# Regrouped columns in tiles of four groups, and batch 0 routed in three parts (512, 1024 and 1024 rows)

## The chip, the cores and the metric

The kernel runs on one core of a Trainium2 chip. The metric is the device time of one execution in microseconds (us), as the median over several runs. A core has a matrix engine (PE, with its weight loads as PEld), a vector engine (DVE), a scalar engine (ACT), a general-purpose engine (POOL) and a queue processor (SP) that issues most transfers. Each engine executes its own instructions strictly in the order of the program and waits for others through semaphores.

## The reference

A Fourier mixing of eight batches, then a mixture of experts in which every row goes to one expert and none is dropped:

```python
X = np.fft.fft(x, axis=1)                 # x: (8, 2496, 256)
x = np.fft.fft(X, axis=2).real.astype(np.float32).reshape(8 * 2496, 256)

logits = x @ w_gate                       # 8 experts
expert_idx = np.argmax(logits, axis=1)
probs = softmax(logits)                   # + 1e-9 in the denominator
gate_w = probs[np.arange(N), expert_idx]
for e in range(8):                        # rows of expert e, w1: (256, 1024), w2: (1024, 256)
    y[rows_e] = np.maximum(x[rows_e] @ w1[e], 0.0) @ w2[e]
return gate_w[:, None] * y
```

## The kernel before, in words

**Transform.** The sequence of 2496 is taken as 104 x 24. `first(b)` does the transforms of length 104 for one batch: it loads the batch in three thirds (`load`, tile `xq`, three buffers), folds each third on DVE (lines 290 to 301), multiplies it on PE (`half1`, PSUM tile `s`), copies the result to SBUF (tile `t`, line 316) and writes it to a scratch array `Td[b]` in DRAM. It has twelve steps. `regroup(b, h)` reads `Td[b]` back with the axes exchanged, as tiles `t4` (the trace calls them `t`). There are eleven groups of 120 columns a batch; before, they come in two tiles, of six groups (768 KB) and five groups (640 KB). `second(b)` does the transforms of length 24 and of the feature axis. Per tile, `turn_last` runs one small matmul (`pr`) and a copy back into `t4` (line 367). Per group, `group` runs two matmuls (the trace calls their PSUM tile `p`, read from `table,t`) and a copy into `zz` (line 374). Then come ten windows of 128 columns: each has two matmuls (PSUM tile `p`, read from `table,zz`), a copy `zs` on ACT (line 400), a copy of the logits `lg` and two operations for 256 finished rows on DVE (lines 403 and 405), and a copy `mirror` on ACT (line 379).

**Routing.** After every half of the windows (five of them, 1280 rows) `route` computes, in 17 small DVE operations, one exponential on ACT and eleven small matmuls (`rk`), the position of every row in a scratch array `Xs` that is sorted by expert. `base` carries the fill of the experts from one part to the next. The rows then wait in a list; each call of `send()` puts one indirect write (128 rows) on POOL's queue (line 230, `Xs<-rows,pi`). A batch needs 20 of them.

**Experts.** `plan` (lines 481 to 514, DVE) turns the fill of the experts into tables of blocks. `experts` is a generator over blocks: `fetch_weights` and `fetch_rows` are issued on SP, `turn` transposes the rows of a block on PE (`pt`, line 571), then come the two products `ph` and `py` (`a` to `e` in a variant with seven products), and POOL writes the rows out. The blocks of round b may start once all rows of batch b have been sent (`whole`). Only then does `fetch_rows` read `Xs`, and it waits for the landing of all indirect writes of that batch.

**Order.** The order of instructions is written out by hand (`tc.manual_schedule()`). After the first stage of batch 0, the program runs the steps of `second(0)` with steps of `early` (the first stage of batch 1) between them and one `send()` after each step; before, seven steps of `early` stand ahead of `second(0)` and one more follows every even step. Then the loop over rounds runs the expert blocks of round b-1 with side steps for batch b: the plan, the second stage of batch b and the first stage of batch b+1. Ahead of the first block lie 18 side steps; they reach the fourth window of batch 1. The PSUM pool `pm_` has three buffers, which `s`, `pr`, `p` and `rk` share.

Of the kernel before, what the change touches and what calls it, by code (L numbers as in the profile page):

```python
# [28 lines left out]
GP = NU * NB  # L29
NP = 112  # L30
NW = -(-NK * NB // 128)
HW = NW // 2
HALF = -(-NG // 2)
LAST = NW * 128 - (NG - 1) * GP
NT = B * S
E, F = 8, 1024
# [2 lines left out]
CAP = NT + BLK  # L39
ROWS = E * CAP + BLK  # L40
W = D + 2
NSL = 2 * HW
NY = H + 1
OUT = 1.0e6

# [11 lines left out]
def shape_consts():  # L57

    c = {}
    n1 = np.arange(NA)[:, None]  # L60
    r = np.arange(NP)
    k1 = r // 2
    im = r % 2

    def wave(n2, f):
        return f(2 * np.pi / S * ((NB * n1 + n2) * k1 % S))

    w1 = [np.where(im, wave(n2, np.sin), wave(n2, np.cos)) for n2 in range(1, NS)]
    for f in (np.cos, np.sin):
        w1 += [np.where(im, 0.0, wave(0, f)), np.where(im, wave(NS, f), 0.0)]  # L70
    c["w1"] = np.stack(w1, 1) * (k1 < NK)

    u, cs, s = np.meshgrid(np.arange(NU), np.arange(2), np.arange(NS), indexing="ij")
    u, cs, s = (v.reshape(-1, 1) for v in (u, cs, s))
    k2 = np.arange(NB)
    t = 2 * np.pi / NB * ((s + 1) * k2 % NB)
    end = np.where(cs, 1.0 - 2.0 * (k2 % 2), 1.0)
    even = np.where(s == NS - 1, end, np.where(cs, -np.sin(t), np.cos(t)))
    odd = np.where(s == NS - 1, end, np.where(cs, np.cos(t), np.sin(t)))
    own = (u == np.arange(NU)).astype(float)  # L80
    c["m2"] = np.stack([(own[:, :, None] * m[:, None, :]).reshape(GP, GP) for m in (even, odd)], 1)

    rot = np.zeros((GP, GP))
    for p in range(GP):
        if p % NS == NS - 1:
            rot[p, p] = 1.0
        elif p // NS % 2:
            rot[p, p - NS] = -1.0
        else:
            rot[p, p + NS] = 1.0  # L90
    c["rot"] = rot

    d = np.arange(H)[:, None]
    m = np.arange(D + 1)
    t = 2 * np.pi / D * (d * m % D)
    rc, rs = np.cos(t), -np.sin(t)
    rs[0] = 1.0 - 2.0 * (m % 2)
    full = np.concatenate([rc[:, :D], rs[:, :D]], 0)


    rd = np.zeros((H, 2, 2 * E + NY + 1))
    sign = 1.0 - 2.0 * (m[:NY] % 2)
    rd[:, 0, 0:NY] = sign * rc[:, 0:NY]
    rs[0] = 0.0
    rd[0, 1, 2 * E] = 1.0
    rd[:, 1, 2 * E + 1:] = sign * rs[:, 0:NY]
    c["rd"] = rd
    c["alt"] = 1.0 - 2.0 * (np.arange(128) % 2)[:, None]
    c["rt"] = full.T.reshape(2, 128, D).transpose(1, 0, 2)

    p = np.arange(128)[:, None, None, None]
    h = np.arange(2)[None, :, None, None]
    g = np.arange(HW)[None, None, :, None]
    mir = np.arange(2)
    tau = 128 * (HW * h + g) + p
    k1 = tau // NB
    k = k1 + NA * (tau % NB)
    bad = (k1 >= NK) | ((mir == 1) & ((k1 == 0) | (k1 == NK - 1)))
    row = np.where(bad, 0, np.where(mir, S - k, k))
    c["row"] = row.reshape(128, 2, NSL)  # L120
    c["good"] = 1.0 - bad.reshape(128, 2, NSL)
    c["far"] = OUT * bad.reshape(128, 2, NSL)
    c["rev"] = np.broadcast_to(E - np.arange(E), (128, E))
    c["cap"] = np.broadcast_to(CAP * np.arange(E), (128, E))
    c["sgn"] = np.where(np.arange(128) == 0, 1.0, -1.0)[:, None]
    c["lane"] = np.arange(128)[:, None]
    c["tri"] = np.triu(np.ones((128, 128)), 1)
    c["ident"] = np.eye(128)
    return {n: np.ascontiguousarray(v, dtype=np.float32) for n, v in c.items()}
# [50 lines left out]
    return todo  # L180


TICKS = 32
LATE = 4
SHARE, ROOM = 0.6, 1.2
# [24 lines left out]
def kernel(ctx: ExitStack, tc, x, w_gate, w1, w2, out):  # L210
# [3 lines left out]
    def mm(o, lhsT, rhs, start=True, stop=True, **kw):  # L214
        nc.tensor.matmul(o, lhsT=lhsT, rhs=rhs, start=start, stop=stop, **kw)  # L215
# [128 lines left out]
    base = con["cap"]  # L344

    def regroup(b, h):
        t4 = sp.tile([128, HALF, D], F32, tag="t4", name="t4")
        n = min(HALF, NG - h * HALF)
        nc.sync.dma_start(
            out=t4[:, 0:n], in_=bass.AP(Td[b].tensor, Td[b].offset + h * HALF * GP * D,  # L350
                                        [[D, 128], [GP * D, n], [1, D]]))
        ahead[b, "t4", h] = t4

# [2 lines left out]
    def second(b):  # L356
# [3 lines left out]
        def turn_last(h):  # L360

            nonlocal t4
            t4 = ahead.pop((b, "t4", h))
            n = min(HALF, NG - h * HALF)
            pr = pm_.tile([GP, HALF], F32, tag="m", name="pr")
            mm(pr[:, 0:n], con["rot"][:], t4[0:GP, 0:n, H])
            act.copy(t4[0:GP, 0:n, H], pr[:, 0:n])  # L367

        def group(g):
            i, n = g % HALF, LAST if g == NG - 1 else GP  # L370
            p2 = pm_.tile([128, 2, n], F32, tag="m", name="p2")
            for c in range(2):
                mm(p2[:, c], t4[0:GP, i, c * H:(c + 1) * H], con["m2"][:, c, 0:n])
            act.copy(zz[:, :, g * GP:g * GP + n], p2[:])
            if g == HALF - 1:
                turn_last(1)

        def mirror(rows, k):
            act.copy(free(rows[:], (k + 1) * W + D - 1, [-W, 2], [-1, H - 1]),
# [5 lines left out]
        yield  # L385
        group(1)
        yield
        for h in range(2):
            rows = sp.tile([128, NSL, W], F32, tag="rows", name="rows")
            lg = sp.tile([128, NSL, E], F32, tag="lg", name="lg")  # L390
            for i in range(HW):
                w, k = HW * h + i, 2 * i
                if w + 2 < NG:
                    group(w + 2)
                p3 = pm_.tile([128, 2 * NY + 2 * E + 1], F32, tag="m", name="p3")
# [8 lines left out]
                for m, op in enumerate((ALU.add, ALU.subtract)):  # L404
                    vec.scalar_tensor_tensor(rows[:, k + m, 0:NY], p3[:, 0:NY], zs[:, 0:1], zs[:, 1:],  # L405
                                             op0=ALU.add, op1=op)
                yield
            mirror(rows, k)
            yield from route(b, h, rows, lg)

    def route(b, h, rows, lg):

        nonlocal base

        def small(name, *dims, dt=F32):
            return sp.tile([128, *dims], dt, tag=name, name=name)

        mx, eq, v = small("mx", NSL), small("eq", NSL, E), small("v", NSL)
        vec.reduce_max(mx[:], lg[:], axis=AX_X)
        vec.tensor_tensor(eq[:], lg[:], bc(mx[:], 2, E), op=ALU.is_equal)  # L420
        vec.tensor_tensor(eq[:], eq[:], bc(con["rev"][:], 1, NSL), op=ALU.mult)
        vec.reduce_max(v[:], eq[:], axis=AX_X)
        vec.tensor_tensor(v[:], v[:], con["good"][:, h], op=ALU.mult)
        oh = small("oh", NSL + 1, E, dt=BF16)
        vec.memset(oh[:, NSL], 0.0)
        vec.tensor_tensor(oh[:, 0:NSL], bc(con["rev"][:], 1, NSL), bc(v[:], 2, E), op=ALU.is_equal)
        yield

        su = small("su", NSL)
        vec.tensor_tensor(lg[:], lg[:], bc(mx[:], 2, E), op=ALU.subtract)  # L430
        act.activation(lg[:], lg[:], ACTF.Exp)
        vec.tensor_scalar(rows[:, :, D], con["row"][:, h], float(b * S), None, op0=ALU.add)
        yield

        rk = pm_.tile([128, NSL + 1, E], F32, tag="m", name="rk")
        mm(rk[:], tri[:], oh[:], True, False)
        for s in range(NSL):
            mm(rk[:, s + 1:], ones[:], bc(oh[:, s], 1, NSL - s), False, s == NSL - 1)
        vec.reduce_sum(su[:], lg[:], axis=AX_X)
        vec.tensor_scalar(su[:], su[:], 1e-9, None, op0=ALU.add)  # L440
        vec.reciprocal(rows[:, :, D + 1], su[:])
        yield

        pos, pf, pi = small("pos", NSL, E), small("pf", NSL), small("pi", NSL, dt=I32)
        vec.tensor_tensor(pos[:], rk[:, 0:NSL], bc(base[:], 1, NSL), op=ALU.add)
        vec.tensor_tensor(pos[:], pos[:], oh[:, 0:NSL], op=ALU.mult)
        vec.reduce_sum(pf[:], pos[:], axis=AX_X)
        vec.tensor_tensor(pf[:] if b >= LATE else pi[:], pf[:], con["far"][:, h], op=ALU.add)
        nxt = cp.tile([128, E], F32, tag="base", name="base", bufs=2)
        vec.tensor_tensor(nxt[:], rk[:, NSL], base[:], op=ALU.add)  # L450
        base = nxt
        for s in range(NSL):
            waiting.append((b, pf[:, s:s + 1], pi[:, s:s + 1], rows[:, s]))

    waiting = deque()
# [302 lines left out]
    def ahead_of(b):  # L758

        yield from first(b)  # L760
        regroup(b, 0)
        regroup(b, 1)

    def mixed(b):

# [32 lines left out]
    load(1, 1)  # L798
    regroup(0, 0)
    regroup(0, 1)  # L800
    load(1, 2)
    nc.sync.dma_start(out=bt[:], in_=const_dram("blocks", cv))
    sent(unordered(nc.sync.dma_start(
# [10 lines left out]
        else:  # L814
            vec.tensor_copy(con["rd"][:, c, to + E:to + 2 * E], pg[:])
    early = ahead_of(1)
    for _ in range(7):
        next(early)
    for k, _ in enumerate(second(0)):
        if k % 2 == 0:  # L820
            next(early, None)
        send()
    work = experts(todo)
# [81 lines left out]
```

## Time and profile before

| what | value |
|---|---|
| median of 7 runs | 1322.09 us (1318.71 to 1324.41) |
| the profiled execution | 1321.24 us |
| its span, first to last instruction | 1319.5 us |
| PE busy | 1273.3 us (96%) |
| DVE / ACT / POOL busy | 581.7 / 374.0 / 329.5 us |
| mean granted PE clock | 0.979 |
| first transposition of expert rows (`pt`) | at 85.69 us |

The profiled execution lasts 1.74 us longer than its span and lies 0.85 us below the median. In the lists of the profile each line is a group of instructions: start, duration, engine, source line, operation, output<-input; in square brackets stands the idle time of the engine ahead of it and what ended it. Matmuls in single precision appear as two instructions each.

### The profile page before, as it was taken

What the parts mean: (1) busy time and instruction counts of PE and PEld (TensorE: products, weight loads), DVE (VectorE), ACT (ScalarE), POOL (GpSimd) and SP (SyncE); (2) the same over time, 40 slices, a digit from 0 to 9 for tenths busy, and PEclk for the clock granted to TensorE, in tenths of its full rate; (3) what the DMA queues carried; (4) which work ended last, traced back from release to release, by engine and by line L of the source; (5) the groups of instructions that cost most, each with busy time, mean ns of one, the idle gap of its engine ahead of it and who ended that gap; (6) DMA issues with size and microseconds to landing.
All of it is one profiled execution on the core that took longest, in us unless ns stands there. A gap on an engine that the chain in (4) does not pass through costs nothing.

```text
span 1319.5 us, 19014 instructions
## 1 busy us (share of the span) xinstructions
PE 1273.3 (96%) x6655; PEld 1102.3 (84%) x6655; DVE 581.7 (44%) x1533; ACT 374.0 (28%) x886; POOL 329.5 (25%) x335
## 2 busy tenths in 40 slices
PE   6769999999999999999999999999999999999998
PEld 4649988776888888888888888888888889999887
DVE  4554253352656535655556643675544421111111
ACT  1422141231244223433334322433322221111111
POOL 0236125043114411143113511153311111111111
PEclk6879999999999999999999999999999999999999
DMA  8878967455436522574333632243422237776784
GB/s 235 271 250 294 393 208 246 161 172 197 169 134 213 189 104 100 177 265 147 125 110 99 225 119 100 100 176 132 164 107 105 102 146 273 253 277 255 270 316 189
DMA packets 63100, 249.63 MB, mean 189 GB/s; under 512 B 10057, under 2 KB 24883, under 8 KB 43420
## 3 DMA queue, kind: packets, MB, share of 16 engines
q1 hardware_dynamic: 46231, 203.33, 43.9%
q0 software_dynamic: 15888, 42.14, 8.8%
q10 hardware_dynamic: 885, 2.94, 0.7%
q8 instruction: 54, 0.88, 0.3%
q14 instruction: 42, 0.34, 0.1%
HBM read 194.97 MB, written 54.83 MB: 189 GB/s over the span
## 4 chain that ended last, share of the span: by engine, by line
PE 89%; issue 2%; DMA 1%; POOL 1%; DVE 1%; ACT 0%; POOLq 0%; SPq 0%; ACTq 0%
PE py L215 41%; PE ph L215 14%; PE a L215 7%; PE c L215 7%; PE p L215 5%; PE d L215 3%; PE b L215 3%; PE e L215 3%; PE pt L571 3%; PE s L215 2%; POOL Xs L230 1%; DMA Xs<-rows,pi 1%; DMA xb<-Xs 0%; PE rk L215 0%; ACT y L721 0%
## 5 line engine op out<-in xcount | busy, mean ns | idle before, releaser
L215 PE MATMUL py<-w_sb,hT 128*128 128x256 f32 x2560 | 578.0, 380 | 0.0
L215 PEld LDWEIGHTS py<-w_sb,hT 128*128 128x128 f32 x2560 | 478.0, 191 | 60.2
L230 POOL DMA_INDIRECT out_dram<-y,ro x163 | 159.3, 977 | 811.8 <-ACT y L721 737.9
L215 PE MATMUL ph<-xT,w_sb 128*128 128x128 f32 (+2 forms) x1216 | 220.3, 338 | 2.9 <-ACT y L721 2.1
L721 ACT ACTIVATE y<-py,xb 128x256 f32<-128x256 f32 x163 | 77.2, 474 | 511.6 <-PE py L215 501.8
L215 PEld LDWEIGHTS ph<-xT,w_sb 128*128 128x128 f32 x1216 | 179.2, 192 | 33.6 <-issue 17.2
L230 POOL DMA_INDIRECT Xs<-rows,pi x160 | 162.1, 1013 | 172.7 <-DVE rows L405 53.4
L698 DVE TENSOR_SCALAR hT<-ph 128x512 f32<-128x512 f32 x63 | 43.5, 691 | 297.1 <-issue 204.9
L604 DVE TENSOR_TENSOR u<-p,b 128x512 f32<-128x512 f32 x50 | 34.4, 687 | 172.1 <-PE b L215 156.6
L215 PE MATMUL a<-xT,w_sb 128*128 128x256 f32 x400 | 102.7, 379 | 0.0
L572 DVE TENSOR_SCALAR xT<-pt,table 128x512 f32<-128x512 f32 (+1 forms) x94 | 63.2, 673 | 49.4 <-PE pt L571 49.3
L215 PEld LDWEIGHTS a<-xT,w_sb 128*128 128x128 f32 x400 | 75.5, 190 | 10.0
L215 PE MATMUL s<-xq,w 104*112 104x256 f32 (+2 forms) x208 | 62.0, 421 | 12.1 <-DVE xq L292 11.6
L700 ACT ACTIVATE hT<-ph 128x512 f32<-128x512 f32 x63 | 37.6, 597 | 115.9 <-PE ph L215 115.9
L614 ACT ACTIVATE hT<-a 128x512 f32<-128x512 f32 x50 | 29.9, 597 | 130.9 <-PE a L215 130.9
L403 DVE COPY lg<-p 128x16 f32<-128x16 f32 x80 | 13.8, 173 | 120.2 <-ACT zs L400 120.2
L571 PE MATMUL pt<-table,xb 128*128 128x128 f32 x326 | 53.3, 279 | 9.4 <-DMA xb<-Xs 9.4
L215 PE MATMUL p<-table,zz 128*128 128x145 f32 (+1 forms) x320 | 56.5, 300 | 5.5 <-DVE rows L405 4.3
L215 PEld LDWEIGHTS p<-table,t 120*128 120x128 f32 x352 | 53.5, 201 | 8.9 <-issue 2.4
L571 PEld LDWEIGHTS pt<-table,xb 128*128 128x128 f32 x326 | 39.0, 142 | 24.2 <-DMA xb<-Xs 10.1
L215 PE MATMUL p<-table,t 120*128 120x120 f32 (+1 forms) x352 | 57.5, 287 | 1.6 <-ACT t L367 1.1
L215 PEld LDWEIGHTS s<-xq,w 104*112 104x112 f32 x208 | 38.8, 204 | 22.7 <-DVE xq L292 10.9
(115 smaller groups left out, 1289.6 us busy)
## 6 DMA issues: line engine op xcount, KB each, us to landing
w_sb<-in_moe_w_dram SPq DMA_DIRECT2D x132, 1024.0 KB, 7.7
xq<-in_x_dram SPq DMA_DIRECT2D x24, 896.0 KB, 8.9
xb<-Xs SPq DMA_DIRECT2D x28, 516.0 KB, 3.7
Td<-t SPq DMA_DIRECT2D x18, 448.0 KB, 3.3
t<-Td SPq DMA_DIRECT2D x8, 768.0 KB, 12.4
t<-Td SPq DMA_DIRECT2D x8, 640.0 KB, 14.0
xb<-Xs SPq DMA_DIRECT2D x13, 258.0 KB, 3.0
xb<-Xs SPq DMA_DIRECT2D x25, 129.0 KB, 3.2
```

Of the source, the lines that this page charges most:

```text
L215: nc.tensor.matmul(o, lhsT=lhsT, rhs=rhs, start=start, stop=stop, **kw)
L230: return unordered(pool.indirect_dma_start(out=dst, out_offset=bass.IndirectOffsetOnAxis(ap=idx, axis=0), in_=rows, in_offset=None, bounds ...
L403: vec.tensor_copy(lg[:, k:k + 2], p3[:, NY:NY + 2 * E].rearrange("p (m e) -> p m e", m=2))
L571: nc.tensor.transpose(pt[:, c, t], xb[:, 2 * h + t, c * 128:(c + 1) * 128], ident[:])
L572: vec.tensor_scalar(xT[:, :, 256 * h:256 * h + 128 * n], pt[:].rearrange("p c t k -> p c (t k)"), con["alt"][:], None, op0=ALU.mult)
L604: vec.tensor_tensor(u2[:], p1[:], b[:], op=add)
L614: act.activation(h11, a[:], ACTF.Relu)
L698: vec.tensor_scalar(o, ph[:], 0.0, None, op0=ALU.max)
L700: act.activation(o, ph[:], ACTF.Relu)
L721: act.activation(y[:], py[:], ACTF.Copy, scale=xb[:, i, D + 1:D + 2])
```

## The change

The regrouped columns come in tiles of four groups (`TG = 4`): three transfers a batch, of 512, 512 and 384 KB, into three buffers of the smaller size, with one `turn_last` for each tile, so three instead of two. Batch 0 is routed in three parts, of two, four and four windows (`PARTS`), where all other batches keep two parts of five. `route` takes the size of its part. The constants `row`, `good` and `far` lose the axis for the half and are cut by column. Six steps of `early` stand ahead of `second(0)` instead of seven, and the even steps 0 and 2 of `second(0)` are no longer followed by one.

```diff
-HALF = -(-NG // 2)
+TG = 4
...
+PARTS = (2, 4, 4)
...
     def regroup(b, h):
-        t4 = sp.tile([128, HALF, D], F32, tag="t4", name="t4")
-        n = min(HALF, NG - h * HALF)
+        t4 = sp.tile([128, TG, D], F32, tag="t4", name="t4", bufs=3)
+        n = min(TG, NG - h * TG)
         nc.sync.dma_start(
-            out=t4[:, 0:n], in_=bass.AP(Td[b].tensor, Td[b].offset + h * HALF * GP * D,
+            out=t4[:, 0:n], in_=bass.AP(Td[b].tensor, Td[b].offset + h * TG * GP * D,
                                         [[D, 128], [GP * D, n], [1, D]]))
...
-            if g == HALF - 1:
-                turn_last(1)
+            if g % TG == TG - 1:
+                turn_last(g // TG + 1)
...
-        for h in range(2):
+        w = 0
+        for part in PARTS if b == 0 else (NW // 2, NW // 2):
             rows = sp.tile([128, NSL, W], F32, tag="rows", name="rows")
             lg = sp.tile([128, NSL, E], F32, tag="lg", name="lg")
-            for i in range(HW):
-                w, k = HW * h + i, 2 * i
+            for i in range(part):
+                k = 2 * i
...
+                w += 1
                 yield
             mirror(rows, k)
-            yield from route(b, h, rows, lg)
+            yield from route(b, slice(2 * (w - part), 2 * w), rows[:, 0:2 * part], lg[:, 0:2 * part])
...
-    def route(b, h, rows, lg):
+    def route(b, at, rows, lg):
         nonlocal base
+        n = at.stop - at.start
...
-        rk = pm_.tile([128, NSL + 1, E], F32, tag="m", name="rk")
+        rk = pm_.tile([128, n + 1, E], F32, tag="m", name="rk")
         mm(rk[:], tri[:], oh[:], True, False)
-        for s in range(NSL):
-            mm(rk[:, s + 1:], ones[:], bc(oh[:, s], 1, NSL - s), False, s == NSL - 1)
+        for s in range(n):
+            mm(rk[:, s + 1:], ones[:], bc(oh[:, s], 1, n - s), False, s == n - 1)
...
-        for s in range(NSL):
+        for s in range(n):
             waiting.append((b, pf[:, s:s + 1], pi[:, s:s + 1], rows[:, s]))
...
     def ahead_of(b):
         yield from first(b)
-        regroup(b, 0)
-        regroup(b, 1)
+        for h in range(-(-NG // TG)):
+            regroup(b, h)
...
     regroup(0, 0)
     regroup(0, 1)
+    regroup(0, 2)
     load(1, 2)
...
     early = ahead_of(1)
-    for _ in range(7):
+    for _ in range(6):
         next(early)
     for k, _ in enumerate(second(0)):
-        if k % 2 == 0:
+        if k % 2 == 0 and k >= 4:
             next(early, None)
         send()
```

More of the change, by code (lines that the diff above doesn't have):

```diff
@@ L31 @@
 NW = -(-NK * NB // 128)
-HW = NW // 2
-HALF = -(-NG // 2)
+TG = 4
 LAST = NW * 128 - (NG - 1) * GP
@@ L41 @@
 W = D + 2
-NSL = 2 * HW
+NSL = 2 * (NW // 2)
 NY = H + 1
@@ L109, in shape_consts @@
     c["rt"] = full.T.reshape(2, 128, D).transpose(1, 0, 2)
-    p = np.arange(128)[:, None, None, None]
-    h = np.arange(2)[None, :, None, None]
-    g = np.arange(HW)[None, None, :, None]
+    p = np.arange(128)[:, None, None]
     mir = np.arange(2)
-    tau = 128 * (HW * h + g) + p
+    tau = 128 * np.arange(NW)[None, :, None] + p
     k1 = tau // NB
@@ L119, in shape_consts @@
     row = np.where(bad, 0, np.where(mir, S - k, k))
-    c["row"] = row.reshape(128, 2, NSL)
-    c["good"] = 1.0 - bad.reshape(128, 2, NSL)
-    c["far"] = OUT * bad.reshape(128, 2, NSL)
+    c["row"] = row.reshape(128, 2 * NW)
+    c["good"] = 1.0 - bad.reshape(128, 2 * NW)
+    c["far"] = OUT * bad.reshape(128, 2 * NW)
     c["rev"] = np.broadcast_to(E - np.arange(E), (128, E))
@@ L363, in turn_last @@
             t4 = ahead.pop((b, "t4", h))
-            n = min(HALF, NG - h * HALF)
-            pr = pm_.tile([GP, HALF], F32, tag="m", name="pr")
+            n = min(TG, NG - h * TG)
+            pr = pm_.tile([GP, TG], F32, tag="m", name="pr")
             mm(pr[:, 0:n], con["rot"][:], t4[0:GP, 0:n, H])
@@ L369, in group @@
         def group(g):
-            i, n = g % HALF, LAST if g == NG - 1 else GP
+            i, n = g % TG, LAST if g == NG - 1 else GP
             p2 = pm_.tile([128, 2, n], F32, tag="m", name="p2")
@@ L406, in second @@
                                              op0=ALU.add, op1=op)
+                w += 1
                 yield
             mirror(rows, k)
-            yield from route(b, h, rows, lg)
-    def route(b, h, rows, lg):
+            yield from route(b, slice(2 * (w - part), 2 * w), rows[:, 0:2 * part], lg[:, 0:2 * part])
+    def route(b, at, rows, lg):
         nonlocal base
+        n = at.stop - at.start
         def small(name, *dims, dt=F32):
             return sp.tile([128, *dims], dt, tag=name, name=name)
[L418 to L421, printed above, removed]
+        mx, eq, v = small("mx", n), small("eq", n, E), small("v", n)
+        vec.reduce_max(mx[:], lg, axis=AX_X)
+        vec.tensor_tensor(eq[:], lg, bc(mx[:], 2, E), op=ALU.is_equal)
+        vec.tensor_tensor(eq[:], eq[:], bc(con["rev"][:], 1, n), op=ALU.mult)
@@ L422, in route @@
         vec.reduce_max(v[:], eq[:], axis=AX_X)
[L423 to L426, printed above, removed]
+        vec.tensor_tensor(v[:], v[:], con["good"][:, at], op=ALU.mult)
+        oh = small("oh", n + 1, E, dt=BF16)
+        vec.memset(oh[:, n], 0.0)
+        vec.tensor_tensor(oh[:, 0:n], bc(con["rev"][:], 1, n), bc(v[:], 2, E), op=ALU.is_equal)
@@ L427, in route @@
         yield
[L429 to L432, printed above, removed]
+        su = small("su", n)
+        vec.tensor_tensor(lg, lg, bc(mx[:], 2, E), op=ALU.subtract)
+        act.activation(lg, lg, ACTF.Exp)
+        vec.tensor_scalar(rows[:, :, D], con["row"][:, at], float(b * S), None, op0=ALU.add)
         yield
-        rk = pm_.tile([128, NSL + 1, E], F32, tag="m", name="rk")
+        rk = pm_.tile([128, n + 1, E], F32, tag="m", name="rk")
@@ L436, in route @@
         mm(rk[:], tri[:], oh[:], True, False)
-        for s in range(NSL):
-            mm(rk[:, s + 1:], ones[:], bc(oh[:, s], 1, NSL - s), False, s == NSL - 1)
-        vec.reduce_sum(su[:], lg[:], axis=AX_X)
+        for s in range(n):
+            mm(rk[:, s + 1:], ones[:], bc(oh[:, s], 1, n - s), False, s == n - 1)
+        vec.reduce_sum(su[:], lg, axis=AX_X)
         vec.tensor_scalar(su[:], su[:], 1e-9, None, op0=ALU.add)
@@ L442, in route @@
         yield
-        pos, pf, pi = small("pos", NSL, E), small("pf", NSL), small("pi", NSL, dt=I32)
-        vec.tensor_tensor(pos[:], rk[:, 0:NSL], bc(base[:], 1, NSL), op=ALU.add)
-        vec.tensor_tensor(pos[:], pos[:], oh[:, 0:NSL], op=ALU.mult)
+        pos, pf, pi = small("pos", n, E), small("pf", n), small("pi", n, dt=I32)
+        vec.tensor_tensor(pos[:], rk[:, 0:n], bc(base[:], 1, n), op=ALU.add)
+        vec.tensor_tensor(pos[:], pos[:], oh[:, 0:n], op=ALU.mult)
         vec.reduce_sum(pf[:], pos[:], axis=AX_X)
-        vec.tensor_tensor(pf[:] if b >= LATE else pi[:], pf[:], con["far"][:, h], op=ALU.add)
+        vec.tensor_tensor(pf[:] if b >= LATE else pi[:], pf[:], con["far"][:, at], op=ALU.add)
         nxt = cp.tile([128, E], F32, tag="base", name="base", bufs=2)
-        vec.tensor_tensor(nxt[:], rk[:, NSL], base[:], op=ALU.add)
+        vec.tensor_tensor(nxt[:], rk[:, n], base[:], op=ALU.add)
         base = nxt
-        for s in range(NSL):
+        for s in range(n):
             waiting.append((b, pf[:, s:s + 1], pi[:, s:s + 1], rows[:, s]))
```

## The prediction

> **What bounds the kernel now.** I read the page first: PE is busy for 1273.3 us of a span of 1319.5, and 89% of the chain that ended last is PE. So only PE's idle time can be won. The second view places it: PE's waits from 90 us to the end (waiter, releaser: us in total, times, longest).
>
> ```profile
> PE pt L571 <- DMA xb<-Xs: 2.6, 1, 2.6
> PE ph L215 <- ACT y L721: 2.1, 3, 0.7
> PE rk L215 <- DVE oh L426: 1.5, 2, 1.3
> PE p L215 <- ACT t L367: 1.1, 5, 0.3
> ```
>
> Together 7.3 us. After 90 us PE is packed: the end moves with the moment at which the first block's transposition starts, and with every instruction that PE gets afterwards. The third view is PE's timeline around that moment.
>
> ```profile
> 77.63 1.32 PE L215 MATMUL p<-table,zz 128*128 128x145 f32 x4
> 85.69 1.12 PE L571 MATMUL pt<-table,xb 128*128 128x128 f32 x4 [6.74 <-DMA xb<-Xs]
> 87.66 3.49 PE L215 MATMUL ph<-xT,w_sb 128*128 128x256 f32 x8 [0.84 <-DVE xT L572]
> ```
>
> PE has finished its side steps at 78.95 and waits 6.74 us for the rows. The chain that ended last says why:
>
> ```profile
> 79.25 0.97 POOL Xs L230
> 80.22 0.30 issue
> 80.53 2.35 DMA Xs<-rows,pi
> ...
> 83.12 2.52 DMA xb<-Xs
> ```
>
> The twentieth indirect write starts at 80.53, lands at 82.88, the fetch lands at 85.65. POOL's timeline shows twenty writes without a hole: 0.97 busy plus 0.30 issue, 1.277 us each, from the first, which waits for the first routing.
>
> ```profile
> 53.85 1.11 POOL L230 DMA_INDIRECT Xs<-rows,pi  x1 [53.40 <-DVE rows L405]
> ...
> 70.22 1.78 POOL L230 DMA_INDIRECT Xs<-rows,pi  x1 [0.30 <-issue]
> ```
>
> 19 x 1.277 = 24.3 would end at 78.1; four stretched writes like the second line (all beside folds on DVE, lines 290 to 301) make the other 2.4. Last, DVE's timeline shows what holds the first routing back:
>
> ```profile
> 40.30 0.29 DVE L290 TENSOR_TENSOR pm<-xq 104x127 f32<-104x127 f32 x1 [8.06 <-DMA xq<-in_x_dram]
> ...
> 43.05 0.17 DVE L403 COPY lg<-p 128x16 f32<-128x16 f32 x1
> ```
>
> DVE stands 8.06 us for the third load of batch 1, folds it (2.75 us), and only then takes window 0, whose matmuls ran at 40.56.
>
> **Start of batch 0's windows.** The first transfer shrinks from 768 to 512 KB. Today `pr` waits for it until 35.07; its issue was at 30.21. From 32 to 40 us the DMA row runs at 302 to 389 GB/s, so 256 KB less is about 0.8 us: `pr` at 34.2. Two `s` groups (2.03 and 1.28 us on PE at 35.49 and 39.01) leave the way to window 0. Window 0's matmuls move from 40.56 to about 37.6, and DVE can take its logits at 39.4 instead of 43.05: 3.7 earlier. The third `regroup` issue on SP (0.5 us, as 30.21 0.99 x2 shows) delays only that third load, which DVE now wants at 41.8 and which lands near 40.7.
>
> **First two windows and a routing (four writes).** Windows 0 and 1 end at 41.8. Then come the moved fold's first part (1.47), the routing and the fold's second part (1.28). Ten-column routing takes 3.5 us (49.37 to 52.91); its 17 operations cost 0.16 to 0.24 us each mostly for being operations, so I take 3.3 with four columns. First positions at 47.4, first write at 48.3 (today 0.93 after the positions), four writes until 53.4.
>
> **Windows 2 to 5 and the second routing.** Four windows at 1.25 us (today 52.91 to 58.11 for five, 1.04 each; an `s` group and a `turn_last` lie between, and the pool's three buffers couple PE to DVE): 52.4. Routing 3.5: 55.9. POOL stands from 53.4; the fifth write starts at 56.5. Sixteen writes, the last 15 x 1.277 = 19.2 later, plus 1.5 to 2.4 of stretching: 77.4 (77.2 to 78.1) instead of 80.53. So the queue itself gains 3.1, not the 5.5 by which it starts earlier.
>
> **Windows 6 to 9, third routing, plan.** 5.0 + 3.5 + small waits: `base` is final at 64.5. Today it is at 61.76. The balance agrees: 3.7 earlier start, less 2.75 of folds moved in, less 3.3 for a third routing, less part of two `s` groups. The third part's `rows` tile takes the first part's buffer, a new wait: DVE's window 6 at 57.6 may not write until the first four writes have landed (start 52.1 plus 2.3 to 6.9, the span of landings from 50 to 84 us: 54.4 to 59.0; I take 57, no cost). Behind it on DVE would stand routing 3 and the plan.
>
> **What the late plan costs.** The plan follows `base`, and SP issues the first block's weights (2 MB) after it: today 69.14, in the changed kernel 69.14 + 2.7 = 71.9. In the DMA row of 68 to 80 us the engines are full from 72.2 to 78.3. Writes that POOL starts meanwhile land late: 72.31 takes 6.25 us, 75.42 4.28, but the last, at 80.53, 2.35. With weights flowing until 81.1, a last write started at 77.4 lands near 82.2, not at 79.8. Plus 2.8 for the fetch: the transposition at 85.0 instead of 85.69. PE's side steps, which DVE drives from the plan on (9.87 of 10.59 us busy from 61.79 to 72.38), end at 78.95 + 2.7 = 81.7 and stay covered; so do `half1` of batch 1's last third, some 6 us later, its write and `regroup(1)`: its first tile lands near 67 (today 62.0), and DVE reaches the first window of batch 1 only near 75. That cover is gone if it lands after 70.5. Head: -0.7.
>
> **What every later batch pays.** One more `pr`: it starts at 680.13 and the next matmul at 680.27, 0.14 us. Six batches behind the packed point: 0.8. The copy back (0.17) delays a following group by up to 0.3 us (last line of the first list); I take 0.4 in all. The extra SP issue, the smaller transfers and batch 1's `pr` lie in idle time. Tail: +1.2 (0.8 to 2.6).
>
> Sum: -0.7 + 1.2 = +0.5: span 1320.0, execution 1321.7 (1.74 outside), and 0.85 up to the median: 1322.6.
>
> **Two rules beside the rows.** Clock: the granted clock is 0.50 from 73.6 to 90.7 and 1.00 after, changing at multiples of 3.4 us, so `ph` x8 takes 3.49 instead of 1.89. I let the start shift with the transposition. The Trainium skill ("TensorE: Matmul & The Clock Gate", Part 1) says that one free-running window of 3.4 us of sustained activity lifts the gate; by it a start earlier by under one window may win nothing or up to 1.7 us, and the sum would be 1320.9 to 1322.6. Transfers: the second tile lands 2.1 us behind the first today, so their fixed parts overlap. The skill ("DMA: Bandwidth & Descriptors", Bandwidth) speaks against this change: make transfers at least 1 MiB. With its fixed 2 us for one more transfer the last tile comes 2 us later, over ten before its use; the sum stays.
>
> **The rivals.** *The early writes pay* (29%): windows at today's 1.04 put the second positions at 55.0, `base` at 63.0, weights end at 79.6 and do not hold the last write (76.3 + 2.35 = 78.7). Transposition at 81.5 or, by PE's side steps (80.2), no earlier: -4.2 + 1.2 = -3.0, 1319.1 (1317.4 to 1320.5 with the clock). For it: DVE stands 8.06 us today. Against it: 3.3 us more routing work on DVE, which is busy for 12.84 of 18.71 us in this stage. *The third routing delays the plan* (29%): one mechanism, `base` later than 66.6, through PE at half clock (from 39.5 to 46.3 the steps above keep it busy for only some 4.0 of 6.8 us; with 3.83 of 6.83 from 53.1 to 60.0 the clock fell to 0.50), or the `rows` wait. At 67.5 the weights end at 84.1, the transposition is at 88.0: +2.3 + 1.2 = 1325.6 (1324 to 1327). Below 66.6 it does not exceed the bound. *As summed* (42%): 1321 to 1324.5. That the change does not do what it says is excluded for order: the engines follow the program.
>
> **How the numbers follow.** About 0.2% (2.6 us: below 1319.5, above 1324.7) is what can be told from no change. Early writes: four fifths are faster; late plan: six sevenths slower; the forecast gives 0.02 faster and 0.05 slower. So 0.25 faster, 0.30 slower, 0.45 neither. The range reaches into both rivals: 1317.8 to 1326.0; the likeliest case's own is 1321 to 1324.5.
>
> **What would show it.** First write near 48.3, a hole on POOL after the fourth, the last near 77.4; the plan's first line near 64.6; weights issued near 71.9; `pt` near 85.0 after an idle time of about 3 us; three `pr` a batch; waits after 90 us near 8 us. It is wrong if `pt` starts below 83 or above 87, or if PE's waits after 90 us grow by over 2 us.

## The result and the profile after

The changed kernel takes 1326.87 us (median of 18 runs, 1323.42 to 1331.52) against 1321.76 for the kernel before (44 runs, 1317.92 to 1326.03). The ratio is 1.0039, with a 95% interval of 1.003 to 1.0048: slower by 5.1 us, where the forecast was +0.5. The profiled execution lies 2.0 us below that median: 1324.87 us, its span 1323.1 against 1319.5.

The page's totals show what cannot explain it. PE's busy time is up by only 1.5 us (1273.3 before).

```profile
PE 1274.8 (96%) x6672; PEld 1106.1 (84%) x6672; DVE 583.7 (44%) x1550; ACT 375.1 (28%) x895; POOL 330.0 (25%) x335
```

The head came as forecast. DVE's timeline shows window 0's logits at 38.23 (forecast 39.4) and the plan's first line at 65.07 (64.6):

```profile
38.23 0.17 DVE L404 COPY lg<-p 128x16 f32<-128x16 f32 x1 [6.37 <-ACT zs L401]
...
65.07 0.15 DVE L484 TENSOR_TENSOR p_nb<-base,bt 1x8 f32<-1x8 f32 x1
```

POOL's timeline has the first write, the hole ahead of the fifth, and the last write (forecast 48.3, 56.5 and 77.4):

```profile
46.84 1.11 POOL L229 DMA_INDIRECT Xs<-rows,pi  x1 [46.38 <-DVE rows L406]
...
56.32 0.97 POOL L229 DMA_INDIRECT Xs<-rows,pi  x1 [4.55 <-ACT t L315]
...
78.45 0.97 POOL L229 DMA_INDIRECT Xs<-rows,pi  x1 [0.30 <-issue]
```

The chain that ended last shows the last write landing late, as forecast: it takes 4.09 us instead of 2.35 and lands at 82.54 (forecast 82.2). The weights moved beside it: their second half, issued at 72.73, took 9.0 us to land. The DMA engines' busy share is 0.72 from 78.45 to 82.54, against 0.27 in the kernel before from 80.53 to 82.88.

```profile
78.45 4.09 DMA Xs<-rows,pi
...
82.78 2.57 DMA xb<-Xs
...
85.40 1.13 PE pt L574 x4
```

So `pt` starts at 85.40 after 3.82 us of idle time (forecast 85.0 and about 3; before, 85.69 and 6.74). The span behind `pt` is the other part: 1237.7 us instead of 1233.8, **3.9 longer**. Part of the answer, 1.6 of the 3.9 us, stands in PE's waits from 90 us to the end:

```profile
PE pt L574 <- DMA xb<-Xs: 2.6, 1, 2.6
PE ph L214 <- ACT y L724: 2.1, 3, 0.7
PE p L214 <- ACT t L367: 1.8, 7, 0.4
PE rk L214 <- DVE oh L429: 1.5, 2, 1.3
PE p L214 <- DVE base L453: 0.6, 3, 0.2
PE p L214 <- ACT zz L374: 0.3, 1, 0.3
```

The first two and the fourth are as before. The others, all ahead of matmuls with the tile `p`, were 1.1 us and are 2.7. Five of them stand ahead of a group's matmuls, as before; the six new ones stand ahead of a window's. PE's timeline of batch 6 shows where a wait of the fifth line lies. Before:

```profile
703.07 0.60 PE L215 MATMUL p<-table,t 120*128 120x120 f32 x4
703.51 0.67 PE L215 MATMUL p<-table,zz 128*128 128x145 f32 x4
704.02 1.06 PE L215 MATMUL s<-xq,w 104*112 104x256 f32 x4
```

After:

```profile
705.98 0.60 PE L214 MATMUL p<-table,t 120*128 120x120 f32 x4
706.42 0.28 PE L214 MATMUL pr<-t,table 120*120 120x3 f32 x2
706.90 0.74 PE L214 MATMUL p<-table,zz 128*128 128x145 f32 x4 [0.20 <-DVE base L453]
707.47 1.03 PE L214 MATMUL s<-xq,w 104*112 104x256 f32 x4
```

Group 7, the added `pr`, window 5: the group ends a tile of four, so the third `turn_last` falls between it and the first window behind a routing. `rk`, the group, `pr` and the window ask one after the other for the pool's three buffers, and here the window waits until DVE has made `base` out of `rk`. From group to `s` it is 1.49 us instead of 0.95. The window behind the third `pr` waits in six of the seven batches: 0.38, 0.38 and 0.34 us in batches 1 to 3 (ended by ACT), 0.20 in each of batches 4 to 6 (ended by `base`), nothing in batch 7. In batch 1 this already lies behind the first `pt`:

```profile
98.31 0.37 PE L214 MATMUL pr<-t,table 120*120 120x3 f32 x2
99.06 0.77 PE L214 MATMUL p<-table,zz 128*128 128x145 f32 x4 [0.38 <-ACT t L367]
```

In batch 2 the wait at this place (0.38 us, ended by ACT) costs more. Before:

```profile
185.16 0.21 PE L215 MATMUL rk<-oh,tri 128*128 128x88 bf16 x1 [1.33 <-DVE oh L426]
...
187.79 1.89 PE L215 MATMUL ph<-xT,w_sb 128*128 128x256 f32 x8
```

After, it comes 1.7 us behind a wait of 1.33 that both kernels have, and the `ph` x8 takes 2.44 instead of 1.89:

```profile
186.25 0.21 PE L214 MATMUL rk<-oh,tri 128*128 128x88 bf16 x1 [1.33 <-DVE oh L429]
...
187.92 1.09 PE L214 MATMUL p<-table,zz 128*128 128x145 f32 x4 [0.38 <-ACT t L367]
188.81 1.91 PE L214 MATMUL s<-xq,w 104*112 104x256 f32 x4
190.51 2.44 PE L214 MATMUL ph<-xT,w_sb 128*128 128x256 f32 x8
```

The table by windows of the same execution (its last three columns are the granted clock, the DMA share and GB/s) shows why they are longer: 3.4 us at a clock of 0.50.

```profile
184.80:188.20 3.40, 1.70 (x20) 1.40 (x20) 3.17 (x16) 1.55 (x5) 0.00 (x0) 1.00 0.95 356
188.20:191.60 3.40, 3.40 (x11) 2.79 (x11) 1.76 (x9) 0.85 (x2) 1.81 (x2) 0.50 0.80 318
191.60:195.00 3.40, 3.40 (x20) 3.12 (x20) 1.38 (x4) 1.02 (x3) 2.48 (x4) 1.00 0.83 243
```

The kernel before runs at 1.00 there, but at 0.50 from 230.7 to 234.1, behind the 2.6 us wait for the second round's rows. The changed kernel's profile has the same wait (2.56 us, until 233.38) and no drop there.

### The profile page after: what moved, and what is told of

Read it like the earlier page. It is cut to its first block, busy times and chain, and to the rows that moved or that the text cites. A ratio compares the mean times of both kernels' runs of the same rounds, so it can differ in the third digit from the quotient of the medians.

```text
span 1323.1 us, 19099 instructions
## 1 busy us (share of the span) xinstructions
PE 1274.8 (96%) x6672; PEld 1106.1 (84%) x6672; DVE 583.7 (44%) x1550; ACT 375.1 (28%) x895; POOL 330.0 (25%) x335
## 4 chain that ended last, share of the span: by engine, by line
PE 89%; DMA 4%; DVE 3%; issue 2%; ACT 1%; POOL 1%; POOLq 0%; SPq 0%; ACTq 0%
PE py L214 40%; PE ph L214 15%; PE a L214 7%; PE c L214 7%; PE p L214 6%; PE e L214 3%; PE d L214 3%; PE b L214 3%; PE pt L574 3%; PE s L214 3%; DMA Td<-t 1%; DMA Xs<-rows,pi 1%; DMA t<-Td 1%; DMA xq<-in_x_dram 1%; DVE xq L300 0%
## 5 line engine op out<-in xcount | busy, mean ns | idle before, releaser
L214 PE MATMUL s<-xq,w 104*112 104x256 f32 (+2 forms) x208 | 58.9, 404 | 13.1 <-DVE xq L291 12.9
```

## The experiments

Theory A: the third turn of batches 1 to 7 makes the loss. Theory B: the early part does (the smaller routing parts, the order, or the small tiles of batch 0). The runs E1 to E16 went to three chips: E1 to E8 to one and E9 to E12 to another, where the kernel before takes 1346.8 to 1348.1 us, E13 to E16 to a third, where it takes 1321.89. Each ratio (with its 95% interval) is against the kernel before on the same chip.

**The change again.** The changed kernel, unedited, as a yardstick for the others.

> The changed kernel once more, beside the others of this group. My theory: about +3.4 us of it is the third turn in seven batches (0.5 us each, seen in every trace with tiles of four), the rest is the head: ratio 1.002 to 1.004. Rival, that the tiles cost nothing: ratio as the parts and the order alone had it, 0.996 to 1.000.

E8, 1354.89 us: 1.0054 (1.0032 to 1.0077).

> The changed kernel once more, as the partner of the three beside it. Both theories: 1.003 to 1.006.

E14, 1328.20 us: 1.0048 (1.0033 to 1.0062). The loss is there on both chips on which the changed kernel was repeated.

**The tiles alone.** Routing and order as before; tiles of four everywhere.

```diff
-PARTS = (2, 4, 4)
+PARTS = (5, 5)
...
-    for _ in range(6):
+    for _ in range(7):
...
-        if k % 2 == 0 and k >= 4:
+        if k % 2 == 0:
```

> The tiles of four groups alone, with the routing in two parts of five windows and the order of before. My theory: the loss lies in the third turn of each batch. It stands in window 5, the first after a routing, where rk, the group, pr and the window claim the three PSUM buffers in one step; the traces put about 0.5 us on each of seven batches, so +3 to +4 us (1324.8 to 1325.8), with PE waits ahead of window 5 in every batch. Rival, that the routing in three parts costs the time at the head: 0 to +0.8 us (1321.8 to 1322.6).

E1, 1351.51 us: 1.0023 (1.0 to 1.0045). In favour of A, but the interval ends at no change.

**Everything but the tiles.** Tiles of six and five groups; parts and order as changed. Run three times.

```diff
-TG = 4
+TG = 6
...
-        t4 = sp.tile([128, TG, D], F32, tag="t4", name="t4", bufs=3)
+        t4 = sp.tile([128, TG, D], F32, tag="t4", name="t4", bufs=2)
...
-    regroup(0, 2)
```

> Routing in parts of 512, 1024 and 1024 rows and the new order, with two tiles of six and five groups. My theory: only the head changes, by -0.5 to +1.5 us (1321.3 to 1323.3); from 240 us on its matmuls keep a constant distance from the kernel before. Rival, that the third routing and its late plan cost the time: +3.5 to +5 us (1325.3 to 1326.8).

E2, 1346.45 us: 0.9976 (0.9953 to 0.9999).

> Two tiles with the parts and the order of the changed kernel, once more, to see whether the head alone gains. My theory: 0.996 to 0.999 of the kernel before. Rival, that its first result was scatter: 0.9995 to 1.001.

E11, 1345.94 us: 1.0002 (0.9983 to 1.0021).

> Two tiles with the parts and the order, for the third time, since 0.9976 and 1.0002 do not settle whether the head gains. My theory: 0.998 to 1.000, and within 0.002 of the kernel with tiles of four in batch 0 alone. Rival, that tiles of four cost at the head: at least 0.002 below that kernel.

E15, 1320.77 us: 0.9999 (0.9984 to 1.0013). The first looked like a gain; the two others do not bear it out. Parts and order together gain nothing and cost nothing that can be measured.

**Order alone and parts alone.** The kernel of the last diff, with `PARTS = (5, 5)`, or with the order of before (seven steps ahead, every even step).

> Two tiles and two routings as before, only the order of batch 1's steps of the changed kernel (six ahead, none after the even steps 0 and 2). My theory: the window 0 of batch 0 starts some 3.5 us earlier, but batch 1's last third, and with it its regrouping, comes later; positions of the first part near 52, so -1 to +1 us (1320.8 to 1322.8). Rival, that the late regrouping of batch 1 costs the time at the head: +2 to +4 us (1323.8 to 1325.8).

E4, 1347.78 us: 0.9996 (0.9977 to 1.0015).

> Two tiles and the order of before (seven steps of batch 1 ahead, one after every even step), with the parts of 512, 1024 and 1024 rows. My theory: DVE still stands until batch 1's last third has landed, so the first write starts near 51 instead of 47 us, and the third routing still delays the plan: 0.999 to 1.002. Rival, that the parts alone bring the head's gain: 0.996 to 0.998.

E12, 1347.83 us: 1.0011 (0.9985 to 1.0037). Neither differs from before. With this B is reduced to the small tiles of batch 0.

**Tiles of four in batch 0 only.** Everything as changed, but batches 1 to 7 keep two tiles and so two turns.

```diff
-TG = 4
...
+    def tg(b):
+        return 4 if b == 0 else 6
...
     def regroup(b, h):
+        TG = tg(b)
+        if h == 2:
+            t4 = bp.tile([128, 3, D], F32, tag="xs", name="t4", bufs=1)
+        else:
+            t4 = sp.tile([128, 6, D], F32, tag="t4", name="t4", bufs=2)
...
```

> The changed kernel with tiles of four in batch 0 alone (its third tile lies in another pool); batches 1 to 7 have two tiles, of six and five groups, again. Head as in the changed kernel, no third turn later. My theory, that the loss is the third turn of batches 1 to 7: 3 to 4 us faster than the changed kernel beside it, ratio 0.999 to 1.002. Rival, that tiles of four cost their time in batch 0: ratio 1.003 to 1.006, as the changed kernel.

E13, 1323.64 us: 1.0018 (1.0003 to 1.0033). This is the separating run: it differs from the changed kernel (1328.20 beside it) by the third turn and third transfer of batches 1 to 7 (and by the buffers that the tiles lie in), and takes **4.6 us less**. It is still 0.4 to 4.4 us above the kernel before, and 2.9 us above E15: 1.0018 against 0.9999, just at the bound of 0.002 that was set between theory and rival for E15. The profiles place this difference mostly in the head, but one profile of each cannot prove it. E13's `pt`, after 4.86 us of idle time:

```profile
87.39 1.11 PE L581 MATMUL pt<-table,xb 128*128 128x128 f32 x4 [4.86 <-DMA xb<-Xs]
```

E15's:

```profile
83.61 1.12 PE L574 MATMUL pt<-table,xb 128*128 128x128 f32 x4 [4.70 <-DMA xb<-Xs]
```

Two things differ in these heads. E13's DVE gets the third load of batch 1 at 41.64 (E14's at 41.88), E15's at 39.40: one transfer more is queued ahead of it. And E15 met a full clock (1.00 from 32 to 36 us; 0.50 in before, the changed kernel and E13). Neither decides alone: E14 has the full clock there too and starts `pt` at 87.53; the changed kernel's first profile has its third load by 40.62. The landing of the last indirect write scatters too: 6.37 us in E13, 4.8 in E15, 5.2 in E14, 4.09 in the changed kernel's first profile. E15's profiled execution is also 2.1 us below its own median. So a part of B, that tiles of four cost up to some 3 us in batch 0, is not excluded, and its cause stays open.

Where the time behind `pt` goes can be read from the timelines. The table takes the start of `rk` in each routing, counts it from the first `pt`, and subtracts the same of the kernel before (us):

| up to | changed | changed (E14) | E13 | E15 | E16 |
|---|---|---|---|---|---|
| batch 1, first routing | 1.07 | 1.16 | 0.22 | 1.17 | 0.54 |
| batch 1, second | 1.58 | 1.68 | 0.23 | 1.17 | 0.54 |
| batch 2, first | 1.38 | 1.48 | 0.23 | 1.17 | 0.47 |
| batch 2, second | 3.57 | 3.68 | 0.24 | 1.17 | 0.47 |
| batch 3, first | 1.67 | 3.15 | -0.14 | -0.92 | 1.30 |
| batch 6, first | 3.19 | 4.68 | -0.14 | -0.93 | 1.92 |
| batch 6, second | 3.72 | 5.20 | -0.13 | -0.91 | 1.93 |
| batch 7, second | 3.92 | 5.40 | -0.13 | -0.92 | 2.13 |
| the end | 3.89 | 5.36 | 0.20 | -0.62 | 2.07 |

The stretch from the first to the second routing of a batch holds the third turn. It gains 0.51 in batch 1, and 0.51 to 0.53 in each of batches 3 to 6 (batch 6: 3.72 - 3.19), 0.21 in batch 7, and 2.19 in batch 2: 0.51, and 1.68 for a window of 3.4 us at half clock. Both profiles of the changed kernel in this table give the same: 3.3 us for seven turns and 1.7 for the clock. A third profile of it, E8's on another chip, has the turns too (0.51 to 0.53 us in batches 1 and 3 to 6, 0.20 in batch 7), but in batch 2 only 0.68 and no drop of the clock. The stretches without a third turn gain nothing, and E13 and E15 gain nothing in any of them. From batch 2 to batch 3 the changed kernel gives back 1.90 in the one profile, which has no drop of the clock near 230 us, and 0.53 in the other, which has one from 235.4 to 238.8. E15, without a third turn, has no drop there either, and gives back 2.09, so this drop does not hang on the third turn.

**One more turn in the kernel before.** Batches 1 to 7 get an unused `pr` and copy behind group 7.

```diff
+    spare = cp.tile([GP, 4], F32, name="spare")
...
+            if b and g == 7:
+                pr = pm_.tile([GP, HALF], F32, tag="m", name="pr")
+                mm(pr[:, 0:3], con["rot"][:], t4[0:GP, 0:3, H])
+                act.copy(spare[:, 0:3], pr[:, 0:3])
```

> The kernel before with one small matmul (120x3) and its copy added after group 7 of batches 1 to 7, where the changed kernel has its third turn; the result of both is not used, the head is untouched. My theory: PE waits for the PSUM buffers ahead of window 5, about 0.5 us a batch: +3 to +4 us, ratio 1.0022 to 1.0030. Rival, that a turn costs only its pitch: +0.14 us a batch, +1.0 us, ratio 1.0007.

E5, 1353.96 us: 1.0052 (1.0031 to 1.0073). One turn, with no transfer, costs as much as the whole change. That is more than the 3 to 4 us I expected. The timeline accounts for 0.51 to 0.54 us a batch and 0.20 in batch 7, some 3.3 in all (batch 2 cannot be told from the scatter of this chip); the interval of the ratio is 4.2 to 9.8 us, so some 0.9 us or more of this run's loss is not explained by the trace. The profiled execution is the fastest of the twelve, 7.6 us below their median.

**Three unused turns, in two places.** The same edit with `for _ in range(3)`, behind group 7 (window 5 follows) or, with `g == 4`, behind group 4 (window 2 follows, no routing near).

> The kernel before with three small matmuls (120x3) and their copies, not used, after group 7 of batches 1 to 7, the place of the changed kernel's third turn. My theory, that a turn there makes PE wait for the three PSUM buffers, 0.5 us or more each: at least three times what one did by the trace, +10 us or more, ratio 1.007 to 1.012. Rival, that a turn costs its pitch of 0.14 us: 21 x 0.14 = +3 us, ratio 1.0022.

E9, 1354.83 us: 1.0066 (1.0045 to 1.0087). That is 8.0 us (6.1 to 11.7) where I expected 10 or more; by the trace three turns cost less than twice as much as one.

> The same three matmuls and copies after group 4, in window 2, where no routing tile holds a buffer of the pool. My theory, that the place matters: about 0.2 us each, as the turn one window earlier showed, +4 us, ratio 1.002 to 1.004, clearly below the run with them in window 5. Rival, that each turn costs the same wherever it stands, because PE waits for ACT's copies in the small pool in either place: the same ratio as in window 5.

E10, 1356.88 us: 1.0073 (1.0053 to 1.0093). I expected the place behind the routing to be the dear one; **this failed.** PE's timelines show where the waits lie. E9, the second `pr` behind the routing:

```profile
580.88 0.55 PE L215 MATMUL pr<-t,table 120*120 120x3 f32 x4 [0.20 <-DVE base L456]
```

E10, the second `pr` in window 2:

```profile
708.64 0.58 PE L215 MATMUL pr<-t,table 120*120 120x3 f32 x4 [0.37 <-ACT spare L382]
```

Here E9's turn waits for `base`, E10's for the turns' own copies (`spare`). Both fit the pool: once its three buffers are in use, a further claim waits until ACT or DVE has emptied the oldest. From batch 5 on it costs 0.91 to 0.95 us a batch behind the routing and 1.2 to 1.4 in window 2. So the routing is only one way to have the buffers taken. No run gave the pool a fourth buffer, which would test this directly.

**The turn one group earlier.** The changed kernel, the next tile's turn behind groups 2 and 6 instead of 3 and 7. No instruction is saved.

```diff
+            t4 = t4s[h] = ahead.pop((b, "t4", h))
...
+            t4 = t4s[g // TG]
...
-            if g % TG == TG - 1:
+            if g % TG == TG - 2 and (g // TG + 1) * TG < NG:
```

> The changed kernel, with the turn of the next tile one group earlier (after groups 2 and 6 instead of 3 and 7), so that none stands in the first window after a routing; same instructions. My theory: the PE waits ahead of window 5 go, and what stays for each pr is 0.14 us: 2 to 3 us faster than the changed kernel (1323.9 to 1324.9). Rival, that the loss is the number of turns or lies at the head: within 0.7 us of the changed kernel (1326.2 to 1327.6).

E3, 1348.96 us: 0.9995 (0.9975 to 1.0014), 5.9 us less than the changed kernel on this chip (E8).

> The changed kernel with its turns one group earlier, once more. By the traces a batch then pays 0.21 us instead of 0.50: my theory 2 us faster than the changed kernel beside it, 1.001 to 1.003; rival, that it is as good as two tiles: 0.998 to 1.000.

E16, 1323.13 us: 1.0009 (0.9994 to 1.0025), **5.1 us less** than the changed kernel beside it, where I had expected 2. PE's timeline of batch 6 has the same `pr` with no wait behind it, at 0.14 us:

```profile
695.98 0.60 PE L214 MATMUL p<-table,t 120*128 120x120 f32 x4
696.42 0.28 PE L214 MATMUL pr<-t,table 120*120 120x3 f32 x2
696.56 0.62 PE L214 MATMUL p<-table,zz 128*128 128x145 f32 x3
```

In the table E16 loses about 0.2 us a batch from batch 3 on (1.30 to 2.13 in four batches), and there is no drop of the clock in batch 2. So what costs is the wait at this place more than the turn itself. How much of the 5.1 us is the clock, the profiles do not settle: between E14's and E16's the time behind `pt` differs by 3.3.

**Two attempts to win more, on parts and order.** E6 issues the second half of the first block's weights behind the block's rows, so that it does not hold the last write back:

```diff
-        nc.sync.dma_start(out=w2_sb[:], in_=w2[ds(ev, 1)].rearrange("o p c d -> p (o c) d"))
+        def rest():
+            nc.sync.dma_start(out=w2_sb[:], in_=w2[ds(ev, 1)].rearrange("o p c d -> p (o c) d"))
...
+                    while held:
+                        held.pop()()
...
```

> Two tiles, the parts and the order of the changed kernel, and in addition the second half of the first block's weights (1 MB) is issued behind its rows instead of ahead of them. My theory, that the weights hold the last indirect writes back: the last write lands some 2 us sooner, unless PE's side steps end last; 0 to 2 us faster than the same kernel without it (0.9961 to 0.9976 of the kernel before). Rival, that nothing waits for these writes any more, or that the second product now waits for its weights: 0.9976 to 0.9990.

E6, 1345.02 us: 0.999 (0.9966 to 1.0013); inconclusive. Its last write, with half of the weights ahead of it, still takes 3.90 us to land. E7 routes batch 0 in other parts, `PARTS = (3, 3, 4)`:

> Two tiles and the order of the changed kernel, with parts of 768, 768 and 1024 rows. My theory, that POOL's queue sets the first block: POOL runs without a hole from about 48 us on, its last write starts 1 to 2 us sooner, 0 to 1.5 us faster than the parts of 512, 1024, 1024 with two tiles (0.9965 to 0.9976 of the kernel before). Rival, that PE's and DVE's side steps set it: no difference (0.997 to 0.998).

E7, 1348.85 us: 1.0027 (1.0006 to 1.0048); worse than the kernel before, where 0.9965 to 0.998 was expected. No version beats the kernel before by more than the measurement can tell.

## Why the prediction was wrong

**Right.** The start of the windows, the hole on POOL, the late plan and the held-back last write came within 1.5 us each, the plan, the weights' issue, the landing and `pt` within 0.5. Both rivals fell: `base` was final at 65.0, not beyond 66.6, and the early writes did not pay, as the last one took 4.09 us to land beside the weights. That the measured 1326.87 lies in the range of the second rival (1324 to 1327) is luck: its late `pt`, 88.0, did not come. The covers held: `regroup(1)`'s first tile was there at 68.2, before DVE reached batch 1's first window at 75.4. The head, forecast at -0.7, was -0.3.

**Less sure than it was put.** The head differs between executions of one kernel: E14 has `pt` at 87.53, 2.1 us after the first profile's 85.40. Its last write started 0.8 us later and took 1.1 us more to land. A head gain of 0.7 is below what one profile can show.

**The step that failed** is "What every later batch pays". It said 0.14 us for a `pr` in six batches and 0.4 in all for the copy back: +1.2, at most 2.6. The runs show that the turn was priced too low, and the profiles show two effects of the clock beside it.

First, the turn itself: 3.3 us instead of 1.2. The price came from a `pr` at a quiet place (680.13 to 680.27). The third `pr` stands elsewhere, behind a routing's `rk` and a group, where the window behind it waits 0.20 to 0.38 us. Batch 1's does not lie in idle time, as the forecast had it: it starts at 98.31, behind `pt`, and costs 0.51. The trace of before had a warning: from the `pr` at 175.67 to the next matmul it is 0.40 us, and from that at 263.51 it is 0.36. Taking the turn out of batches 1 to 7 (E13) recovers 4.6 us; moving it by one group (E16), 5.1.

Second, the clock in batch 2: 1.7 us in the first profile and in E14's, none in E8's nor in E13, E15 and E16. The prediction had no term for a clock that drops behind `pt`. It can be offset: in the first profile the drop near 230 us is missing. How often each happens in unprofiled runs stays open.

Third, the clock's return. After 90 us the forecast let the start shift with `pt`. The clock came back at 92.6 instead of 90.7, though `pt` was 0.3 earlier: +1.07 in the table. The same offset is 1.16 in E14, 1.17 in E15, 0.54 in E16 and 0.22 in E13, so it does not come from the third turn, which E13, E15 and E16 lack or place elsewhere. This agrees with the rule that the prediction set beside the row: the Trainium skill ("TensorE: Matmul & The Clock Gate", Part 1) has the gate judge activity in free-running windows. The bound of 1.7 us, an estimate that the prediction worked out from it, covers all five.

In the profile: -0.3 + 1.07 + 3.3 + 1.7 - 1.9 - 0.3 (the small rest of the table) = 3.6, the difference of the spans. The medians' 5.1 lies between this profile and E14's (+7.2). Of that, the turns' 3.3 us stand in every profile of the changed kernel; how the rest divides between the clock and the head stays open.

The test "waits after 90 us grow by over 2" did not catch it. They grew by 1.6, from 7.3 to 8.9: added instructions and time at half clock do not count as waits.

## What to carry to other kernels

Price an added step on a packed engine at the place where it will stand: count the claims on a shared pool just ahead of it, not the instruction's pitch at a quiet place. Where it falls next to a wait, move it by one step before giving it up; here that recovered 5 us and saved no instruction. And a small gain ahead of a stretch at half clock should be counted as nothing until it is seen: here the clock's return moved by up to 1.2 us against the first block between the profiled executions.

## What the runs showed of the hardware

- The granted clock changed on a grid of 3.41 us: in the profile of before, its rise at 90.7 and its drop at 230.7 lie 41 such windows apart.
- After waits of 1.33 us and 0.38 us in one window (184.8 to 188.2) the granted clock was 0.50 for the next (188.2 to 191.6). The Trainium skill ("TensorE: Matmul & The Clock Gate", Part 1) lets the clock fall after an idle window of about 3.4 us; no wait here was that long. Nor does PE's busy time in a window decide alone: in this profile 1.71 us of 3.41 (184.79 to 188.20) was followed by a drop, 1.67 of 3.41 (229.16 to 232.57) was not.
- A wait of the same length need not act alike: before's 2.6 us wait for the second round's rows lies in one window (PE busy for 0.77 us of it, 227.29 to 230.70) and a drop follows; the changed kernel's 2.56 us lie in two (1.67 and 2.61 busy), and none follows.
- The last indirect write took 2.35 us to land with the DMA engines' busy share at 0.27 (before), and 4.09 with it at 0.72 (changed).
- The kernel before takes 1322 us on one chip and 1347 to 1348 on two others. The difference lies early: E15 and E11 are the same kernel, and from 100 to 500 us PE is busy for 395.8 and 379.1 us of the 400. The runs do not show why.
